# Tiles of 256 tokens with two neighbours in a partition, in a linear-attention and long-convolution kernel on one core

## The chip, the core and the metric

The kernel runs on one core of a Trainium2 chip. The core has five engines that run their own instruction queues and meet at semaphores: PE (TensorE, matrix products into PSUM), DVE (VectorE), ACT (ScalarE), POOL (GpSimd) and SP (SyncE, which here only issues DMAs). PSUM has eight banks of 512 fp32 columns in 128 partitions. DMA transfers are issued from the queues of SP and POOL. The metric is device microseconds of one execution; lower is better.

## The reference

A gated linear attention over 4 batches, 8 heads, 768 tokens and 48 channels, followed by a gated convolution over the whole sequence and a projection (d_model = 384 = 8 x 48):

```python
for t in range(S):
    cur = np.einsum('bhd,bhe->bhde', u[None] * kt, vt)
    y[:, :, t] = np.einsum('bhd,bhde->bhe', rt, state + cur)
    state = wt[:, :, :, None] * state + np.einsum('bhd,bhe->bhde', kt, vt)
...
x = attn_out.transpose(0, 2, 1, 3).reshape(B, S, H * D)
proj = x @ w_proj
x1, x2, x3 = (proj[..., :D].copy(), proj[..., D:2 * D].copy(), proj[..., 2 * D:].copy())
X2 = np.fft.rfft(x2, n=S, axis=1)
H = np.fft.rfft(filter_fft, n=S, axis=0)[None, :, :]
x2_conv = np.fft.irfft(X2 * H, n=S, axis=1)
y = x1 * x2_conv * x3
return (y @ w_out).astype(np.float32)
```

The term with `u` is the bonus: for each token and head it is a sum over the 48 channels of r*k*u, times v. All inputs and the output are fp32.

## The kernel before

The kernel has two stages for each of the four batches.

**First stage, by chunks of 128 tokens** (24 chunks, one token in a partition; `group` and `first`). w, r, k and v of a chunk are loaded by one DMA each, `[L, H, D]`, so each packet is one token of one head, 48 x 4 = 192 bytes (line 1438; twelve loads of v go through POOL's queue and are cast on the way, line 1435). ACT takes the logarithm of w (`ln`, line 1444), PE sums it over the tokens with two triangular masks (`cs`, lines 1473 to 1476), ACT takes exponentials in place in PSUM (`ex`, line 1482; `ph`, line 1493, for the decay over the chunk), and DVE multiplies them into k and r at once (`kq`, 768 columns, helper line 1328). PE turns the result (`tr`, line 1501; two heads to a transpose, each padded to 64 rows), ACT or DVE copies it to SBUF (`qk`), or SP turns it by DMA (line 1507, for the last eight chunks only, `late`). PE then forms the scores (`sc`, line 1519), which are masked by DVE in one product (`mt`, line 1535), or copied by ACT and cut by POOL (`mc`, line 1540). The state goes through PSUM: `ki` (line 1566) adds the old one by the identity, `kv` (line 1560) adds k times v, `su` (line 1570) applies the decay. The output of the chunk is a sum in PSUM of the bonus (`yi`, line 1580, by the identity; or it is added by DVE, line 1609), of r times state (`ys`, line 1589), and of masked scores times v (`yy`, line 1597). It is copied (`xn`), turned (`yt`, line 1621) and stored as `xT`, channels in partitions. The bonus's sum over the channels is made outside PE: `rk` (r*k), `ru` (times u), `rh` (first half plus second half) and a reduction `cc` (line 1458), then `vc` = v times it.

**Second stage, by batch** (`second`): gates x1 and x3 (`p`, `q`, line 1768), the side that is convolved (`xw`, line 1809), the forward transform of the sums and differences of its two halves (`sd`, `f`, line 1655), products with the filter's spectrum (`u`, `p`), the inverse transform (`E`, line 1865), whose even and odd parts are added and subtracted (`aE`, lines 1903 and 1908; `dE`, line 1918), the gate (`yE`), the output projection (`o`, line 1950) and the store (`so`, line 1966). The spectrum of the filter is made once. `PE`, `FOLD` are two ways of the inverse: with both halves in PE, or folded with a `dE` on DVE or POOL.

**Order.** The functions only declare operations with the engines that may do them; the order of all work, the engine of each operation and its PSUM bank stand in one list, `ORDER`, read line by line by `Plan.run`: name, engine (P, A, D, G, S; `-` leaves a variant out), bank. Each engine's queue is in this order; semaphores follow from the data. A last word on a line ties a POOL operation to a DVE operation that it must follow. `warm n bank` issues n filler products whose results are not used (line 1380); there are 93 such units.

Of the kernel before, what the change touches and what calls it, by code (L numbers as in the profile page):

```python
# [15 lines left out]
AX = mybir.AxisListType  # L16
# [4 lines left out]
L = 128  # L21
NCH = S // L
# [6 lines left out]
QT = HALF // 2  # L29
MID = (HALF - 1) / 4  # L30
NC = B * NCH
UNIT = 65536.0

PE, ACT, DVE, POOL, SP, NONE = "P", "A", "D", "G", "S", "-"


ADD, DVE2, ACT2, POOL2, FOLD, WIDE = "V", "M", "N", "C", "Q", "X"

NLW, NLD, NG, NF, NS, NX, NO = 3, 4, 3, 4, 3, 3, 4
CASTS = (2,4,6,8,10,12,)  # L40
NV, NVL = 6, 3
NTURN = 8
NE = 2


# [3 lines left out]
warm 16 4  # L49
first A  # L50
imaps G
smalls D
zeros D
pads D
signs D
lw0 S
lw3 S
kz1 D
ln0 A
maske G  # L60
lw2 S
lr0 S
u S
maskn G smalls
maps G
ang2 D
ia0.0 G
ia1.0 G
maski G
kz0 G pads  # L70
ang1 D
ang0 D
ia2.0 D
cs0 P 2
lk0 S
ln2 A
ex0 A
ew0 -
kq0 D
warm 8 0  # L80
warm 6 1
cs3 P 0
ex3 -
ia2.1 D
kw0 -
lw1 S
ur A
warm 4 5
um P 6
warm 5 5  # L90
tr0 P 4
lk3 S
lr3 S
ew3 X
lr1 S
lk1 S
kz2 G
ph0 A
ub A
ln1 A  # L100
lv0 S
rk0 G ang0
kz3 G kq0
ru0 G
rh0 D
cc0 D
qk0 A
kq3 -
kw3 G rh0
lv2 G cc0  # L110
warm 3 5
cs1 P 5
warm 3 7
sc0 P 3
mt0.1 D
mc0.1 -
lr2 S
lk2 S
vb0 G
vc0 G rh0  # L120
ex1 A
ph3 A
mt0.0 D
ew1 -
lv3 G
warm 3 7
cs2 P 0
warm 4 7
tr3 P 4
ex2 A  # L130
kq1 D
qk3 A
kw1 -
warm 2 7
tr1 P 7
mc0.0 -
rk1 D
ru1 D
rh1 G rk1
qk1 D  # L140
ph1 A
warm 3 2
sc3 P 4
kv0 P 2
su0 D
ew2 -
kq2 D
kw2 -
lv1 S
warm 2 3  # L150
sc1 P 6
yi0 P 2
y0 P
mt1.1 D
lw4 S
mt3.1 -
xn0 A
xa0 -
mt3.0 N
ph2 A  # L160
rk2 D
ru2 D
rh2 G rk2
vb1 A
tr2 P 3
warm 3 2
ki1 P 5
warm 2 2
kv1 P
lw5 S  # L170
lk4 S
lr4 S
qk2 A
ln3 A
mt1.0 D
cc1 D
yt0 P 2
lr5 S
lk5 S
lv5 S  # L180
warm 3 4
sc2 P 0
su1 D
warm 1 3
ki2 P 5
kv2 P
cc2 D
su2 D
cs4 P 6
ex4 A  # L190
wproj1 G
mc3.1 -
ki3 P 4
kv3 P
mt2.1 A
mc1.1 -
ia0.1 G
vc1 D
xT0 D
warm 2 3  # L200
yi1 P 2
ys1 P
vc2 G
mt2.0 D
mc1.0 -
y1 P
ew4 -
su3 D
mc2.1 G mt1.0
kq4 D  # L210
mc2.0 -
cs5 P 0
xn1 A
ex5 A
warm 1 4
yi2 P 3
ys2 P
y2 P
kw4 -
kq5 D  # L220
ew5 -
lw7 S
ph4 A
xn2 A
tr4 P 6
xa1 -
xa2 -
kw5 -
qk4 D
yt1 P 3  # L230
tr5 P 2
yi3 P 6
qk5 D
yt2 P 4
ph5 A
wproj0 G kq4
mc3.0 C
lv4 S
xT2 D
ys3 P  # L240
lr7 S
y3 P
xn3 D
sc4 P 4
mt4.0 D
xa3 -
trig A
sin2 A
rk3 G qk4
ru3 G qk5  # L250
warm 1 0
yt3 P 7
xT1 D
mt4.1 A
ia1.1 G mt4.0
warm 3 0
sc5 P 5
mt5.1 -
lw6 S
mt5.0 M  # L260
xw0.0 P 0
rh3 D
cc3 D
vb3 G rh3
sin1 A
vc3 G mt5.0
ki4 P 2
cxw0.0 D
xT3 A
warm 1 3  # L270
xw0.2 P 6
sin0 A
kv4 P
is A
cxw0.2 D
su4 D
warm 5 4
p0.2.0 P 5
p0.0.0 P 0
table A  # L280
lr6 S
lk6 S
lk7 S
mc4.1 G
filt S
lw8 S
lw9 S
cp0.0.0 D
yi4 P 6
yi5 P 2  # L290
ys5 P
lv7 G cxw0.2
mc5.0 -
mc5.1 -
ys4 P
y5 P
lk9 S
lk8 S
mc4.0 -
y4 P  # L300
xn4 D
if1 A
ln4 A
xn5 A
lv8 S
cs6 P 0
xa5 -
yt5 P 3
if0 A
ex6 A  # L310
lr9 S
xa4 -
yt4 P 2
xT5 D
xT4 D
cs7 P 6
ew6 -
kq6 D
ex7 A
ew7 -  # L320
xw0.4 P 2
lr8 S
kq7 D
ph6 A
cxw0.4 A
sd0.1.0 D
kw7 -
sd0.0.0 D
rk4 G
p0.2.1 P 4  # L330
cp0.2.1 A
ph7 A
kw6 -
lw10 S
p0.0.1 P 0
tr7 P 3
qk7 D
fsd0 D
fsd1 D
tr6 P 7  # L340
ru4 D
cp0.0.1 A
qk6 A
cp0.2.0 A
lv9 S
f0.2 P 0
cf0.2 A
sc6 P 6
mt6.1 -
mc6.1 -  # L350
mt6.0 N
f0.0 P 4
sc7 P 2
cf0.0 A
warm 2 0
h1 P 0
ln5 A
lv6 G sd0.1.0
h2 P 6
rh4 G fsd1  # L360
mt7.1 -
mt7.0 M
mc7.0 -
hc1 A
mc7.1 -
cc4 D
h0 P 2
hc2 A
kv6 P 4
hg1 D  # L370
hg2 D
hc0 A
cs8 P 0
su6 D
mc6.0 C
vc4 G
warm 2 5
yi6 P 6
y6 P
ex8 A  # L380
ew8 -
hg0 D
xn6 A
yi7 P 4
ys7 P
y7 P
xn7 A
xa7 -
xa6 -
cs9 P 6  # L390
kq8 D
yt6 P 3
ki7 P 2
kv7 P
su7 D
wproj2 G
yt7 P 4
xT7 D
ex9 A
xT6 A  # L400
kq9 D
kw8 -
rk5 G
ph8 A
ru5 D
rh5 D
cc5 D
ew9 -
tr8 P 5
ki8 P 2  # L410
qk8 A
ph9 A
vb5 G xT7
vc5 G
xw1.0 P 0
cxw1.0 A
kw9 -
tr9 P 3
qk9 A
kv8 P  # L420
sc8 P 4
su8 D
mt8.1 -
lw11 S
f0.1 P 0
ki9 P 6
kv9 P
mt8.0 M
if2 A
lk10 S  # L430
lk13 S
mc8.0 -
cf0.1 A
sc9 P 2
su9 D
q0.2.1 P 7
lr10 S
mt9.0 N
lk11 S
lr11 S  # L440
mt9.1 -
mc9.1 -
q0.0.1 P 5
lr13 S
yi9 P 0
q0.2.0 P 4
yi8 P 2
xq0.0.1 -
u10.0 D
lw12 S  # L450
ys9 P
ln6 A
ys8 P
cq0.0.1 D
lw13 S
mc8.1 -
y8 P
lv11 G su9
mc9.0 C
warm 5 2 192  # L460
y9 P
cs10 P 5
lr12 S
lv12 S
xq0.2.1 -
u00.0 D
xq0.2.0 -
xn8 A
xn9 A
q0.0.0 P 2  # L470
cq0.2.0 D
cq0.2.1 D
xq0.0.0 -
xa8 -
lk12 S
lv10 G
rk6 G
cq0.0.0 D
xa9 -
gq0.0.0 -  # L480
yt9 P 4
ex10 A
xT9 A
ru6 D
kq10 D
yt8 P 7
xT8 A
cs11 P 0
ex11 A
if3 A  # L490
kq11 D
warm 1 4
xw1.2 P 2
ew10 -
kw10 -
lk15 S
lv13 S
rh6 G ru6
cc6 D
ph10 A  # L500
lr15 S
gq0.2.0 -
lw15 S
lr14 S
p1.2.0 P 4
tr10 P 7
p1.0.0 P 5
cxw1.2 A
qk10 A
ew11 -  # L510
kw11 -
ph11 A
cp1.2.0 A
cp1.0.0 A
tr11 P 2
q1.0.0 P 0
ki10 P 3
sc10 P 4
xq1.0.0 -
ln7 A  # L520
p0.0 D
lw14 S
mt10.1 A
gq0.0.1 -
qk11 D
sc11 P 6
kv10 P
lv15 G
mt11.0 A
vc6 G  # L530
mc10.1 G kq11
mc11.0 G qk11
q1.2.0 P 2
xq1.2.0 -
cq1.0.0 D
mt10.0 D
mt11.1 D
cs12 P 0
rk7 G qk11
ru7 G  # L540
yi10 P 4
ex12 A
ew12 -
su10 D
lv19 G qk11
ys10 P
mc10.0 -
y10 P
lv14 G
mc11.1 -  # L550
cs13 P 6
gq0.2.1 -
# [1496 lines left out]
```

## Time and profile before

| | before |
|---|---|
| median of 3 runs | 158.71 us (158.08 to 159.05) |
| span of the profiled execution | 155.3 us; its own time was not recorded apart from the runs |
| busy, DVE / ACT / POOL | 135.5 / 117.5 / 102.0 us |
| PE products / DVE / ACT / POOL instructions | 1634 / 258 / 195 / 106 |
| HBM read and written | 22.41 and 4.72 MB |

The runs lie 2.8 to 3.8 us above the span, which goes from the first to the last instruction. The profile's page gives the load of each engine in 40 slices of the span, the chain of work that ended last, and the instructions grouped by line and shape. In a group's row, "xN | busy, mean" are the number of instructions, the time in which at least one of them ran, and the mean length of one; after the second bar stands the idle time of the engine just before them and what ended it. PE's products overlap, so their lengths add up to more than the time they take; the timeline gives their starts.

### The profile page before, as it was taken

Reading aid. Unit: us, or ns where it says so; the run is one execution under the profiler, and the core shown is the slowest. Engines: PE = TensorE matmul, PEld = TensorE weight load, DVE = VectorE, ACT = ScalarE, POOL = GpSimd, SP = SyncE. Lnnn points to the kernel's source line nnn. Section 1 sums busy time; section 2 is a strip of 40 time slices with the busy share of each in tenths; the row PEclk is TensorE's granted clock in tenths of the full one; section 3 lists DMA queues with packets and bytes.
Section 4 is the critical chain, followed back from the end, with each engine's and each line's share of the span. In section 5 each row is a group of like instructions: output and inputs, shape, how many; then the busy total and the mean of one; then the engine's idle time right before and its main releaser. Section 6 shows DMA issues by size and latency. Waiting matters only on the chain.

```text
span 155.3 us, 4220 instructions
## 1 busy us (share of the span) xinstructions
PE 142.3 (92%) x1634; PEld 89.4 (58%) x1634; DVE 135.5 (87%) x258; ACT 117.5 (76%) x195; POOL 102.0 (66%) x106
## 2 busy tenths in 40 slices
PE   7999894999999999999799999999999997999860
PEld 2455554656646767666566676665666664666430
DVE  4849984696999998999999999999999988799950
ACT  4584774897899894999879989989965575667650
POOL 6679595968229479589957988678796650802600
PEclk9999999699999999999999999999999999999997
DMA  5999999979999999899999918999997535000784
GB/s 105 227 212 218 194 145 215 200 135 339 177 187 213 198 181 180 142 199 176 187 192 201 179 25 144 220 193 189 178 183 149 155 122 209 0 0 34 294 330 159
DMA packets 112534, 27.12 MB, mean 175 GB/s; under 512 B 108545, under 2 KB 111106, under 8 KB 112514
## 3 DMA queue, kind: packets, MB, share of 16 engines
q1 hardware_dynamic: 98434, 24.49, 73.9%
q0 software_dynamic: 14080, 2.36, 20.0%
q8 instruction: 13, 0.21, 0.6%
q14 instruction: 7, 0.06, 0.1%
HBM read 22.41 MB, written 4.72 MB: 175 GB/s over the span
## 4 chain that ended last, share of the span: by engine, by line
PE 65%; DVE 11%; DMA 9%; ACT 4%; SPq 4%; issue 2%; DVEq 0%; ACTq 0%
PE banks L1768 13%; PE banks L1655 10%; PE banks L1380 7%; PE banks L1809 6%; PE banks L1950 5%; DMA kr<-in_k_dram 4%; PE banks L1865 4%; PE banks L1501 4%; SPq L1438 4%; PE banks L1519 4%; PE banks L1597 3%; DMA w<-in_w_dram 3%; DMA xT<-xn 3%; PE banks L1589 2%; PE banks L1473 2%
## 5 line engine op out<-in xcount | busy, mean ns | idle before, releaser
L1768 PE MATMUL banks<-xT,wproj 128*128 128x384 bf16 x144 | 27.3, 326 | 1.1 <-DVE xT L1334 1.0
L1328 DVE TENSOR_TENSOR kq<-banks,kr 128x768 bf16<-128x768 f32 x23 | 21.6, 950 | 3.1 <-DMA kr<-in_k_dram 2.7
L1328 POOL TENSOR_TENSOR vc<-vb,cc 128x768 bf16<-128x768 bf16 (+1 forms) x12 | 18.7, 1562 | 6.0 <-DVE sd L1820 3.1
L1328 POOL TENSOR_TENSOR rk<-kr 128x768 bf16<-128x768 f32 (+1 forms) x11 | 19.5, 1773 | 4.1 <-DMA kr<-in_k_dram 2.1
L1332 ACT ACTIVATE x<-banks 128x768 bf16<-128x768 f32 (+1 forms) x26 | 17.5, 687 | 5.2 <-PE banks L1809 3.0
L1482 ACT ACTIVATE banks<-banks 128x768 f32<-128x768 f32 x23 | 18.2, 798 | 1.9 <-PE banks L1476 1.6
L1535 DVE TENSOR_TENSOR mt<-banks,mask_excl 128x512 bf16<-128x512 f32 (+1 forms) x24 | 18.1, 772 | 1.3 <-PE banks L1519 1.1
L1768 PEld LDWEIGHTS <-wproj 128*128 128x128 bf16 x144 | 13.5, 98 | 9.3 <-issue 1.2
L1380 PE MATMUL banks<-wt 128*128 128x512 bf16 (+1 forms) x56 | 16.9, 397 | 1.1 <-DVE scl L1394 1.1
L1809 PE MATMUL banks<-wproj,xT 128*128 128x384 bf16 x72 | 13.7, 326 | 1.5 <-DMA xT<-xn 1.0
L1435 POOL DMA_DIRECT2D vb<-in_v_dram x12 | 11.3, 938 | 4.6 <-DVE sd L1820 3.3
L1540 POOL TENSOR_SCALAR_AFFINE_SELECT mt<-mt 128x512 bf16<-128x512 bf16 (+1 forms) x14 | 11.6, 834 | 3.5 <-ACT mt L1332 3.5
L1950 PE MATMUL banks<-wout,y 128*128 128x384 bf16 x72 | 13.3, 326 | 0.7 <-DVE y L1328 0.4
L1655 PE MATMUL banks<-sd,F 128*128 128x384 bf16 (+1 forms) x96 | 13.7, 328 | 0.0
L1501 PE MATMUL banks<-ident,kq 128*128 128x128 bf16 x144 | 11.1, 222 | 2.6 <-DVE kq L1328 2.1
L1332 ACT ACTIVATE qk<-banks 128x1024 bf16<-128x1024 bf16 x12 | 12.3, 1023 | 1.1 <-PE banks L1501 0.9
L1444 ACT ACTIVATE lg<-w 128x768 bf16<-128x768 f32 (+1 forms) x13 | 10.4, 798 | 3.2 <-DMA w<-in_w_dram 3.1
L1455 POOL TENSOR_TENSOR rk<-rk 128x384 bf16<-128x384 bf16 (+1 forms) x8 | 7.4, 921 | 7.7 <-DVE rk L1328 7.6
L1332 ACT ACTIVATE X<-banks 128x768 bf16<-128x768 f32 x12 | 9.8, 815 | 3.0 <-PE banks L1655 2.9
L1501 PEld LDWEIGHTS <-kq 128*128 128x128 bf16 x144 | 9.0, 98 | 4.9 <-DVE kq L1328 2.9
L1655 PEld LDWEIGHTS <-F 128*128 128x128 bf16 (+1 forms) x120 | 8.4, 103 | 5.6 <-issue 1.0
L1328 DVE TENSOR_TENSOR U<-X,hh 128x2304 bf16<-128x2304 bf16 (+1 forms) x12 | 11.6, 982 | 0.0
(118 smaller groups left out, 338.3 us busy)
## 6 DMA issues: line engine op xcount, KB each, us to landing
w<-in_w_dram SPq DMA_DIRECT2D x24, 192.0 KB, 4.2
kr<-in_r_dram SPq DMA_DIRECT2D x24, 192.0 KB, 4.5
kr<-in_k_dram SPq DMA_DIRECT2D x24, 192.0 KB, 4.5
out_dram<-o SPq DMA_DIRECT2D x9, 384.0 KB, 2.9
v<-in_v_dram SPq DMA_DIRECT2D x12, 192.0 KB, 4.0
vb<-in_v_dram POOLq DMA_DIRECT2D x12, 96.0 KB, 5.5
U<-in_moe_filter_fft_dram SPq DMA_DIRECT2D x1, 1152.0 KB, 6.0
wproj<-in_moe_w_proj_dram POOLq DMA_DIRECT2D x3, 288.0 KB, 5.1
```

The source lines that it names most:

```text
L1328: return eng(e).tensor_mul(o, a, b)
L1332: return nc.scalar.activation(out=o, in_=a, func=AF.Copy)
L1380: nc.tensor.matmul(banks[:, at, lo:hi], wt[:, 0:L], x, start=True, stop=True)
L1435: op(f"lv{i}", [POOL], lambda e, bk, q=q, rw=rw: nc.gpsimd.dma_start(out=vb[fv][:, q], in_=v[b, :, rw, :].rearrange("h t d -> t h d")), w= ...
L1482: return nc.scalar.activation(out=o, in_=x, func=AF.Exp)
L1501: nc.tensor.transpose(p[:, HP * m + j, :], kq[f][:, m, 2 * j:2 * j + 2, :], ident)
L1535: return copy(ACT, o, x) if e in (ACT, ACT2) else nc.vector.tensor_mul(o, x, _mid(mask_excl, z - HP * a))
L1540: return nc.gpsimd.affine_select(out=o, in_=o, pattern=[[0, z - HP * a], [1, L]], compare_op=ALU.is_gt, fill=0.0, base=0, channel_multipli ...
L1655: nc.tensor.matmul(p[rows], F[:, ti, c0 + rows.start:c0 + rows.stop], x[q][:, ti, :], start=(ti == 0), stop=(ti == NT - 1),)
L1768: nc.tensor.matmul(p, wproj[:, cb, col0:col0 + L], xT[bx][:, cb, sl], start=(cb == 0), stop=(cb == CB - 1),)
L1809: nc.tensor.matmul(view(bk)[:, z], xT[bx][:, cb, (c0 + z) * L:(c0 + z + 1) * L], wproj[:, cb, C:2 * C], start=(cb == 0), stop=(cb == CB - 1),)
L1950: nc.tensor.matmul(view(bk)[:, z], yt_[:, z, :], wout[:, cb, :], start=(cb == 0), stop=(cb == CB - 1),)
```

## The change

- A tile holds 256 tokens (12 pairs, function `pair` in place of `group` and `first`), two neighbouring tokens j = 0, 1 in each partition. A load of w, r, k or v is then one DMA of 1024 packets of 2 x 48 x 4 = 384 bytes; no load of v is cast on the way.
- A partition group of 64 holds a chunk of 128 tokens: partitions 0 to 63 the first chunk, 64 to 127 the second. The running sums need the even and odd token apart: DVE or POOL forms w_even * w_odd (`ws`), the masks `before` and `upto` are block-diagonal 64 x 64, and `cs` is four wide products for 256 tokens (six for the one pair without `ws`), in three banks.
- k is scaled by exp of the negative sums from SBUF (`ek`, `km`, on DVE or POOL), q from PSUM (`eq`, `qm`).
- State, state read, scores and bonus are products with 64 rows and 64 columns of the array; masked scores times v have 64 rows and 128 columns. There are twice as many of each per token, of the same width (scores: 128 columns, half of which are the even and half the odd tokens).
- The bonus: r*k (`rk`) is turned (`rp` on PE and `rt` as a copy, or `rt` by DMA), and six products with a matrix of u and zeros give its sums over the channels (`cp`, copied by `cc`). `ru`, `rh` and the reduction go.
- The masking is one product on DVE, from PSUM (15 of 24) or from a copy made by ACT (9).
- Turns by DMA: 16 of 24 output tiles, 13 sets of q or k, 4 of r*k (before: 5 and 6).
- The second stage keeps its form; its sequence axis is ordered with even tokens first and odd tokens second (`j`), through gates, inverse tables and output; the forward tables are made for the new order of rows. The gates may be copied by ACT and multiplied from SBUF. Eight of nine inverse sums of the first three batches are folded, before four.
- The order list is new. The tables of sines and the loading of ACT's function tables stand ahead of the first logarithm. There are 49 filler units, 43 of them ahead of the first `cs`.

The core of the diff:

```diff
-    wl = tiles(NLW, [L, 2, H, D], FP32, "w")
-    kr = tiles(NLD, [L, 2, 2, H, D], FP32, "kr")
+    wl = tiles(NW, [L, H, 2, D], FP32, "w")
+    kr = tiles(NR, [L, 2, H, 2, D], FP32, "kr")
...
+        def load(name, t, x, key):
+            op(f"l{name}{gi}", [SP], lambda e, bk: nc.sync.dma_start(
+                out=t.rearrange("p h j d -> p h (j d)"),
+                in_=x[b, :, rows, :].rearrange("h (p j) d -> p h (j d)", j=2)), w=[key], q=(1024, 384))
...
+            if both(bk):
+                sums = (((before, le), (before, ls)), ((upto, le), (before, ls)), ((upto, le), (upto, ls)))
+            else:
+                sums = (((before, ls),), ((before, ls), (ident, le)), ((upto, ls),))
...
-                    nc.tensor.matmul(
-                        p[:, par, j, :], qk[f][p0:p0 + D, j, :], qk[f][p0:p0 + D, HP + j, :],
-                        start=True, stop=True,
-                    )
+                                nc.tensor.matmul(
+                                    p[spans[c], par, i, jk, :].rearrange("p (j t) -> p j t", j=2),
+                                    qkk[x, 0, jk, 2 * a + i, spans[c]], qkk[x, 1, :, 2 * a + i, spans[c]],
+                                    start=True, stop=True,
+                                )
...
+                                nc.tensor.matmul(
+                                    kvp(bk)[spans[par], hp, :], kqq[spans[c], 0, j, h, :], vbb[spans[c], h, j, :],
+                                    start=(ci == 0 and hp == 0 and j == 0), stop=(hp == HP - 1 and j == 1),
+                                )
...
+                                nc.tensor.matmul(
+                                    yview(bk, c)[spans[j], par, hp, :], qkk[x, 1, j, hp, spans[c]], stt[so][x, hp, :],
+                                    start=hp == 0, stop=False,
+                                )
...
+                            nc.tensor.matmul(
+                                yview(bk, c)[:, par, hp, :], mt[sm][spans[c], a, par, q, jk, :],
+                                vbb[spans[c], 2 * hp + par, jk, :],
+                                start=(pi == 0 and c == 0 and hp == 0 and jk == 0), stop=False,
+                            )
...
+        def bonus(e, bk):
+            p = one(bk, f"cp{gi}")[:, 0:2 * H]
+            for n in range(6):
+                nc.tensor.matmul(p, rt[srk][:, n, :], u_b[:, n, :], start=n == 0, stop=n == 5)
```

2759 lines of the change are left out of this document (1288 added, 1471 removed).

## The prediction

> **What bounds the kernel now.** I read the page first, for the loads of the engines and of the transfer queues.
>
> ```profile
> span 155.3 us, 4220 instructions
> PE 142.3 (92%) x1634; PEld 89.4 (58%) x1634; DVE 135.5 (87%) x258; ACT 117.5 (76%) x195; POOL 102.0 (66%) x106
> ...
> PEclk9999999699999999999999999999999999999997
> DMA  5999999979999999899999918999997535000784
> ...
> q1 hardware_dynamic: 98434, 24.49, 73.9%
> q0 software_dynamic: 14080, 2.36, 20.0%
> ```
>
> Three resources are nearly full at once: PE, DVE and, until about 120 us, the DMA engines, which are kept busy by small packets (112,514 packets for 27 MB). A share over the span does not say which one sets the end, so I took the busy time by stage next, for everything and then for line 1380 alone, the filler products ("warm") whose results nobody reads.
>
> ```profile
> 0.00:32.00 32.00, 27.80 (x295) 15.82 (x296) 23.25 (x66) 21.05 (x35) 24.16 (x42) 0.95 1.12 191
> 32.00:150.00 118.00, 114.36 (x1339) 73.62 (x1338) 111.65 (x192) 95.87 (x161) 77.89 (x64) 1.00 0.92 168
> 150.00:156.00 6.00, 0.18 (x2) 0.00 (x0) 0.56 (x1) 0.54 (x1) 0.00 (x0) 0.75 0.49 189
> ```
>
> ```profile
> 0.00:32.00 32.00, 14.06 (x44) 4.10 (x44) 0.95 1.12 191
> 32.00:150.00 118.00, 2.85 (x12) 1.00 (x12) 1.00 0.92 168
> ```
>
> The columns are PE, PEld, DVE, ACT, POOL, the granted clock, the DMA share and GB/s; the second block has PE and PEld only. Without filler PE does 27.80 - 14.06 = 13.7 us of work in the first 32 us, 114.36 - 2.85 = 111.5 us in the next 118, and nothing to speak of in the last 5.1 us (from 150.2 to 155.3), which are the last copies and the store. That is 125.4 us of real PE work. So the run is a start of 32 us that is mostly waiting, a dense stage in which PE works 94.5% and DVE 94.6% of the time, and a fixed end. What counts is PE's real work, how early it becomes dense, and how dense it can stay.
>
> **PE's products, priced.** A busy PE overlaps its products, so I price them from start to start in the timeline (columns: start, length, count).
>
> ```profile
> 36.04 0.37 PE L1589 MATMUL banks<-S,qk 48*128 48x48 bf16 x16
> 36.34 0.57 PE L1597 MATMUL banks<-vb,mt 128*128 128x48 bf16 x16
> 36.83 0.34 PE L1473 MATMUL banks<-lg,mask_neg 128*128 128x384 bf16 x1
> ...
> 37.30 0.61 PE L1621 MATMUL banks<-ident,xn 128*128 128x128 bf16 x6
> ...
> 52.48 1.14 PE L1809 MATMUL banks<-wproj,xT 128*128 128x384 bf16 x6
> 53.46 0.61 PE L1501 MATMUL banks<-ident,kq 128*128 128x128 bf16 x8
> 54.00 0.31 PE L1560 MATMUL banks<-vb,kq 128*64 128x48 bf16 x8
> 54.24 0.40 PE L1519 MATMUL banks<-qk 48*128 48x128 bf16 x8
> 54.57 1.17 PE L1655 MATMUL banks<-sd,F 128*64 128x384 bf16 x12
> ```
>
> A 384-wide product costs 0.98/6 = 0.163 us, a transpose 0.54/8 = 0.067, the running sums of a chunk (cs) 37.30 - 36.83 = 0.47. The small ones: state into kv 0.24 for 8, scores 0.33 for 8, state read (ys) 0.30 for 16, mask times v (yy) 0.49 for 16. A whole-array product of 48 columns thus takes 31 ns, one on half of the rows 19 ns: halves do overlap. No row shows a product on a quarter of the array.
>
> The change per 256 tokens. cs: four wide and four narrow products for two chunks' eight and eight: about 0.65 + 0.14 = 0.79 instead of 0.94; times 12, plus 0.5 for the one pair that sums both tokens on PE, -1.3. Transposes of q and k: 11 sets of eight are left on PE of 18, -7 x 0.54 = -3.8; of the output, 8 sets of three instead of 19, -11 x 0.20 = -2.2; new ones of r*k for the bonus, 8 x 6 x 0.067 = +3.2; the bonus sums, 72 narrow products at about 0.035 (the four narrow ones are the last 0.14 of cs), +2.5. The state product becomes 16 small products for 8, on one half of the rows and alternating column halves as now: between 0.24 (all hidden) and 0.48 (doubled); I take 0.37, since the pace within a run of eight is below the 0.03 that includes the change of shape: 20 x 0.13 = +2.6. ys becomes 16 for 8: 0.30 by its own row against 0.20 (0.30 less half of sixteen at that pace, and the change of shape stays), 20 x 0.10 = +2.0; bounds 0 and +5.8 (31 ns each). Scores: 16 quarter products for 8 half ones, on four quarters that write different banks or halves of them; I take the same 0.33, as for halves the pace halved with the part of the array; bounds 0 and 24 x 0.21 = +5. yy: 32 half products for 16 whole ones, same 0.49; upper bound +5.9. The bonus added by the identity: 24 wide-equivalents at 0.08 to 0.12 for 32, -0.8; if its quarters do not overlap, +1.9. The inverse transform: four of nine that were six 384-wide sums go folded (two 384, four 192 wide), 4 x 2 x 0.163 = -1.3. The sum is -1.3 - 3.8 - 2.2 + 3.2 + 2.5 + 2.6 + 2.0 - 0.8 - 1.3 = +0.9: PE's real work stays at **126.3 us**, with bounds of about 122 and 145. Sixteen of the 24 output transposes and 17 others move to DMA, so PE is where the gain is spent again.
>
> **DVE, ACT, POOL, DMA.** Grouped by form:
>
> ```profile
> L1328 DVE TENSOR_TENSOR kq<-banks,kr 128x768 bf16<-128x768 f32 x23 | 21.6, 950 | 3.1 <-DMA kr<-in_k_dram 2.7 <-ACT banks L1482 0.2
> L1535 DVE TENSOR_TENSOR mt<-banks,mask_excl 128x512 bf16<-128x512 f32 x20 | 13.2, 682 | 0.4 <-PE banks L1519 0.4
> ...
> L1458 DVE TENSOR_REDUCE cc<-rk 128x16 f32<-128x384 bf16 x11 | 6.0, 545 | 0.1
> ...
> L1535 DVE TENSOR_TENSOR mt<-banks,mask_excl 128x1024 bf16<-128x1024 f32 x4 | 4.9, 1221 | 0.9 <-PE banks L1519 0.7
> ...
> L1328 DVE TENSOR_TENSOR y<-y,g 128x768 bf16<-128x768 bf16 x8 | 4.5, 598 | 0.0
> L1328 DVE TENSOR_TENSOR rk<-rk,u_b 128x768 bf16<-128x768 bf16 x7 | 4.5, 640 | 0.0
> ...
> L1455 DVE TENSOR_TENSOR rk<-rk 128x384 bf16<-128x384 bf16 x4 | 3.1, 769 | 0.0
> ...
> L1328 DVE TENSOR_TENSOR rk<-kr 128x768 bf16<-128x768 f32 x1 | 0.9, 948 | 0.0
> ```
>
> DVE: q and k scaling 16 products of 768 for 23, -7 x 0.95 = -6.7 (eight more go to POOL). Masking 15 of 1024 from PSUM (1.22) and 9 from SBUF (about 0.72, the 598 ns row taken to 1024) = 24.8 for 13.2 + 4.9 = 18.1, +6.7. The bonus by VectorE goes (4.5 + 3.1 + 6.0), and four turns of about 0.5 and two tiny copies come, -11.3. Five more r*k, +4.7. Gating mostly from SBUF, about -4; fewer turns and copies, about -7; nine more foldings at 0.35, +3.2; squares of w, flips and small ones, +5. About **-9 us**. ACT gains 14 gating copies (about 9) and casts of v, loses turns and flips: about +5. POOL loses the masking, the bonus and the twelve casting loads: down by some 20.
>
> DMA: 48 loads of 1024 packets of 384 B for 96 of 192 B. A packet now costs 0.739 x 155.3 x 16 / 98434 = 18.7 ns of an engine; the twelve loads of the first batch then need between 14.4 us (same price per packet) and 24.7 us (4.72 MB at the 191 GB/s of the first stage). I take 17, nearer to the packet's price, since the share is full at only 191 GB/s. The 2.7 us that DVE waits for k in the row above go. The cover would be gone only above 25 us, because by then ACT is later, as follows.
>
> **The start.** Rows for ACT:
>
> ```profile
> L1482 ACT ACTIVATE banks<-banks 128x768 f32<-128x768 f32 x23 | 18.2, 798 | 1.9 <-PE banks L1476 1.6
> L1332 ACT ACTIVATE qk<-banks 128x1024 bf16<-128x1024 bf16 x12 | 12.3, 1023 | 1.1 <-PE banks L1501 0.9
> ...
> L1672 ACT ACTIVATE F<-o,mpi 128x768 bf16<-128x768 uint16 x3 | 2.8, 931 | 0.0
> ...
> L1661 ACT ACT_TABLE_LOAD x1 | 1.3, 1283 | 0.8 <-PEq L2033 0.8
> ```
>
> The trigonometric tables move to the front: three table loads (3.85), three sines (2.8) and a wide one (about 1.3) from 0.8 us on, and some waiting for DVE's angles, so the first logarithm starts at about 9.5 us; PE fills that with 22 warm products. Up to the first product of the second stage ACT then does 12 logarithms and exponentials at about 0.8 (9.6), 4 small ones (0.7), 6 turns at 1.02 (6.1), three of 768 (2.4), a mask copy (1.0), three casts (2.5), and three copies and three tiny ones (2.0): 24.3, less 0.05 of overlap for each of 35, 22.5. The second stage starts at 32.0 plus 1.5 of waits, 33.5 us, hardly other than now. But ahead of it stand in the new order the products of three whole pairs and of much of the fourth, by the prices above 20.4 us against 13.7 now, and ACT's 8 us of tables are behind it. Fillers go from 93 to 49 units, 43 of them before the first sum. The row of the clock has one slice at 0.6 now, in the start; two such slices of 3.9 us would cost the new start 3 us, which I keep for the range only, because PE has 20.4 us of work there.
>
> **The sum.** 126.3 - 20.4 = 105.9 us of PE work are left at 33.5 us. DVE has 9 us less to do, POOL 20, DMA is free; ACT's share stays near 81%. I let PE work 96% of the time instead of 94.5%: 110.3 us. With the end of 5.1 us the span is 33.5 + 110.3 + 5.1 = 148.9 us. The runs (158.08 to 159.05, median 158.71) lie 3.4 us above the profiled span, so the time is 152.3, **152 us**.
>
> **The rivals.**
> *Better than that*: quarters overlap four deep and PE's work falls to 122; at 98% in the dense stage that is 33.5 + 103.7 + 8.5 = 145.7 us. 8%.
> *The gain is hidden or given back, about 159*: either only two of four quarters run together (scores +5, identity +1.9, 7 / 0.96 = 7.3, 159.6), or the turns by DMA come late:
>
> ```profile
> xT<-xn SPq DMA_TRANSPOSE x5, 3.9
> ```
>
> SP's queue holds loads and turns in one order, so a turn that waits for its xn holds the loads behind it; three batches that each wait 2.4 us for their last turn give 159.5. Against it: other batches' work stands between. 13%.
> *Slower, by banks*: a pair holds four PSUM banks from its first state read until its output copies, its sums take three and each half of its scores two, where eight exist and a chunk now needs two, two and two. PE then waits for the mask product of 1.22 us that frees the scores. One us in each of 12 pairs gives 164; it decides above 0.7 us a pair. For it: PE already waits nowhere long, so the order is tight; against it: DVE has more room. 13%.
> *Slower, by small products*: every small product costs a whole one's 31 ns: state 0.49 (+2.4), ys 0.49 (+3.8), scores (+3.8), yy 0.98 (+5.9), together 15.9 / 0.96 = 16.6, 169 us. The 19 ns of ys speak against it. 8%. [...]
>
> **Chances.** Forecast 58%. One per cent is about what a measurement of this kernel can tell from no change: 157.1 to 160.3. Faster 58 + 8 = 66%, the same 11% of the 13, slower 2 + 13 + 8 = 23%. The range of 146 to 164 leaves out most of the better case, the 169 and the upper half of the banks' case, about 20%; the forecast's own range is 146 to 157.
>
> **What would show it.** Right: real PE work (without line of the warm products) of 122 to 130 us; 16 scores in 0.3 to 0.4 us from start to start; DVE near 127; first logarithm near 9.5 us, second stage near 33.5; DMA share well below 0.9. Wrong: PE idle before scores or state reads for a mask product (banks), for xT (turns), small products at 25 to 31 ns each, or a second stage that begins after 38 us.

## The result: slower by 8%, and the profile after

| | forecast | before | after |
|---|---|---|---|
| time, median of the runs (us) | 152 | 158.45 (158.08 to 159.05) | 171.84 (169.48 to 176.97) |
| ratio to before, 95% interval | 0.96 | | 1.080 (1.071 to 1.089) |
| start: time without real PE work, up to the first product of the second stage (us) | 13.1 | 18.0 | 15.2 |
| PE's real work (us) | 126.3 | 125.4 | 133.1 |
| dense stage: time without real PE work (us) | 4.4 | 6.8 | 16.2 |
| end, after PE's last product (us) | 5.1 | 5.1 | 5.7 |
| span of the profiled execution (us) | 148.9 | 155.3 | 170.2 |

The profiled execution of the changed kernel took 171.99 us, 1.8 us more than its span. Runs more than 1.5% above a kernel's fastest are left out of every ratio here, so that a ratio can be missing or differ from that of the medians. Each experiment's ratio is to the kernel before as it ran in the same session (medians of 158.77 to 160.66 us); the changed kernel itself was timed in one session only, the one of this table.

The page of the changed kernel, engines and slices:

```profile
span 170.2 us, 5650 instructions
...
PE 140.2 (82%) x2371; PEld 90.2 (53%) x2371; DVE 128.7 (76%) x248; ACT 123.3 (72%) x196; POOL 75.8 (45%) x84
...
PEclk9978997899999999699999999999659999999997
DMA  5999979976999999989899999999912201321884
```

DVE and POOL have less to do than before, ACT about as much as foretold, and every engine works a smaller share. Ahead of the end the granted clock dips in seven slices instead of one, and the DMA engines are nearly full up to 123 us. The stages, split at the first product of the second stage and at PE's last product (columns: stretch, length, PE's busy time and products, clock, DMA share, GB/s), after, and its filler products alone:

```profile
0.00:39.68 39.68, 30.82 (x658) 0.91 0.91 238
39.68:164.50 124.82, 109.39 (x1714) 0.96 0.81 173
164.50:170.20 5.70, 0.00 (x0) 0.80 0.54 174
```

```profile
0.00:39.68 39.68, 6.29 (x22) 0.91 0.91 238
39.68:164.50 124.82, 0.81 (x3) 0.96 0.81 173
```

The same two for the kernel before:

```profile
0.00:30.65 30.65, 26.46 (x288) 0.94 1.12 189
30.65:150.20 119.55, 115.88 (x1351) 1.00 0.92 169
```

```profile
0.00:30.65 30.65, 13.79 (x43) 0.94 1.12 189
30.65:150.20 119.55, 3.12 (x13) 1.00 0.92 169
```

Real work is the first number less the fillers: 24.53 us in the start and 108.58 in the dense stage, where 124.82 us pass; PE is 87.0% dense there. Before it was 112.76 in 119.55, 94.3%. The table is made of these rows. (In the kernel before, real products start while a filler's recorded time still runs, so that this subtraction is some 2 to 5 us too large there; the runs without fillers below have the work with nothing to subtract.) Against the forecast's span 21.3 us are lost: 11.8 as waits in the dense stage, 6.8 as longer PE work, 2.1 in the start, 0.6 at the end.

What PE waits for in the changed kernel (engine and line, what ended the wait: us in total, times, longest). Line 1286 is the product of q (`qm`), 1258 the running sums (`cs`), 1333 the sums of the bonus, 1381 the state reads (`ys`), 1400 the scores, 1631 the gates:

```profile
PE banks L1258 <- DVE kq L1286: 5.8, 5, 2.4
PE banks L1258 <- ACT lg L1245: 3.4, 1, 3.4
PE banks L1333 <- DMA rt<-rk: 3.2, 1, 3.2
PE banks L1381 <- DVE kq L1286: 2.3, 2, 1.4
PE banks L1381 <- issue: 1.9, 1, 1.9
PE banks L1631 <- DVE kq L1286: 1.7, 2, 1.2
PE banks L1400 <- DMA qk<-kq: 0.8, 1, 0.8
...
PE banks L1631 <- DVE mt L1084: 0.4, 1, 0.4
```

The q product ends 9.8 us of PE's waits, 8.0 of them in the dense stage, the mask product 0.4, turns by DMA 4.0. PE never waits for a turned output (`xT`). Three of the longest groups of the kernel before, whose one long wait (1.83 us) lies in the start:

```profile
PE banks L1501 <- DVE kq L1328: 2.1, 2, 1.8
...
PE banks L1809 <- DMA xT<-xn: 1.0, 1, 1.0
PE banks L1768 <- DVE xT L1334: 1.0, 1, 1.0
```

The longest wait for the q product, in the timeline (start, length, instruction, and in brackets the idle time before it):

```profile
64.37 0.80 ACT L1276 ACTIVATE banks<-banks 128x768 f32<-128x768 f32 x1
...
65.16 0.95 DVE L1084 TENSOR_TENSOR kq<-xk,kr 128x768 bf16<-128x768 f32 x1
...
66.03 0.95 DVE L1089 CAST X<-banks 128x768 bf16<-128x768 f32 x1
...
66.89 0.95 DVE L1286 TENSOR_TENSOR kq<-banks,kr 128x768 bf16<-128x768 f32 x1
67.14 1.81 POOL L1084 TENSOR_TENSOR rk<-kr 128x768 bf16<-128x768 f32 x1
67.89 0.49 PE L1258 MATMUL banks<-lg,before 128*128 128x384 bf16 x2 [2.43 <-DVE kq L1286]
```

The sums of pair 7 take the three banks of pair 6 (`cs6 P 4` and `cs7 P 4` in the order list; so do pairs 4 and 5, 8 and 9, 10 and 11). They are free when q of pair 6 has been multiplied out of them. Its exponential ends at 65.17 us, but DVE has two other instructions in its queue first (65.16 and 66.03 us), and PE, for which these sums come next in the list, stands for 2.43 us.

In this trace the granted clock is 1.00 or 0.50, and its records last 3.41 us or a multiple of that (up to 47.79 us). Three pairs of neighbouring windows of 3.41 us (PE's busy time and products, clock, DMA share, GB/s; the page shows 1.00 ahead of the first record of the clock, which begins at 4.13 us here):

```profile
7.54:10.96 3.42, 0.13 (x1) 1.00 1.07 285
10.96:14.37 3.41, 3.41 (x24) 0.50 1.11 304
65.57:68.98 3.41, 1.08 (x24) 1.00 0.93 229
68.98:72.40 3.42, 3.42 (x34) 0.50 1.34 156
116.77:120.18 3.41, 1.82 (x69) 1.00 1.43 178
120.18:123.60 3.42, 1.84 (x27) 0.50 0.95 195
```

After each of these windows, in which PE worked little, comes one at half clock: behind the start, behind the wait just shown, and in one of 3.2 us for the last turn of r*k. There are five ahead of PE's last product, before there was one. The other two begin at 123.60 us, after the window at 120.18, and at 28.02, after a window in which PE was busy for 2.50 of 3.41 us, with 117 small products; so PE's busy time alone does not sort the windows, and a later run comes back to it. The longest pause of PE in the first window of the second pair was 2.43 us. The trace puts 15.3 us of real PE work into the five windows. A wide product of the sums takes 0.32 us from start to start there (30.04 to 30.36 us) and 0.16 at full clock (68.38 to 68.54), 32 products of masked scores and v 0.75 (123.31 to 124.06) and 0.50 (below). By the author's estimate, with everything taken to double as the wide ones do, half of the 15.3, 7.7 us, is what the windows add, against 1.8 before, and at full clock PE's work is 133.1 - 7.7 = 125.4 us.

The small products, by their starts:

```profile
55.05 0.44 PE L1381 MATMUL banks<-S,qk 48*64 48x48 bf16 x32
55.31 0.41 PE L1400 MATMUL banks<-qk 48*64 48x128 bf16 x16
55.65 0.66 PE L1486 MATMUL banks<-sd,F 128*128 128x384 bf16 x3
```

```profile
40.81 0.57 PE L1422 MATMUL banks<-vb,mt 64*128 64x48 bf16 x32
41.31 0.36 PE L1436 MATMUL banks<-vc,ident 64*64 64x192 bf16 x8
```

32 state reads in 0.26 us (8 ns each), 16 scores in 0.34, 32 products of scores and v in 0.50. The transfers that turn tiles (count, median from issue to landing):

```profile
xT<-xn SPq DMA_TRANSPOSE x16, 3.3
qk<-kq SPq DMA_TRANSPOSE x13, 4.6
rt<-rk SPq DMA_TRANSPOSE x4, 4.2
```

33 turns for 11. Added up over the trace's packets, the work of the 16 DMA engines on loads of w, r, k and v fell from 109.1 to 75.6 us, that on turns rose from 11.0 to 36.9.

### The profile page after: what moved, and what is told of

Read it like the earlier page. It is cut to its first block, busy times and chain, and to the rows that moved or that the text cites. A ratio compares the mean times of both kernels' runs of the same rounds, so it can differ in the third digit from the quotient of the medians.

```text
span 170.2 us, 5650 instructions
## 1 busy us (share of the span) xinstructions
PE 140.2 (82%) x2371; PEld 90.2 (53%) x2371; DVE 128.7 (76%) x248; ACT 123.3 (72%) x196; POOL 75.8 (45%) x84
## 4 chain that ended last, share of the span: by engine, by line
PE 34%; DVE 13%; DMA 4%; ACT 2%; issue 2%; SPq 1%; ACTq 0%; DVEq 0%
PE banks L1631 8%; PE banks L1793 7%; PE banks L1486 7%; PE banks L1722 4%; DMA rt<-rk 4%; DVE U L1084 3%; DVE kq L1286 3%; PE banks L1655 2%; DVE mt L1084 2%; PE banks L1258 1%; DVE P L1695 1%; PE banks L1422 1%; DVE sd L1667 1%; DVE S L1372 1%; PE banks L1361 1%
## 5 line engine op out<-in xcount | busy, mean ns | idle before, releaser
L1084 DVE TENSOR_TENSOR mt<-banks,causal 128x1024 bf16<-128x1024 f32 x15 | 18.1, 1218 | 6.2 <-PE banks L1400 6.2
L1084 POOL TENSOR_TENSOR vc<-vb,cc 128x768 bf16<-128x768 bf16 x10 | 14.7, 1474 | 16.6 <-ACT xn L1088 10.2
L1084 POOL TENSOR_TENSOR kq<-xk,kr 128x768 bf16<-128x768 f32 x8 | 14.5, 1810 | 16.7 <-DVE U L1084 12.2
L1267 ACT ACTIVATE xk<-banks 128x768 f32<-128x768 f32 x12 | 9.7, 812 | 7.7 <-PE banks L1262 7.7
L1793 PE MATMUL banks<-wout,y 128*128 128x384 bf16 (+1 forms) x78 | 13.3, 327 | 0.0
L1286 DVE TENSOR_TENSOR kq<-banks,kr 128x768 bf16<-128x768 f32 x12 | 11.4, 951 | 1.6 <-ACT banks L1276 1.5
L1088 ACT ACTIVATE o<-banks 128x768 f32<-128x768 f32 (+1 forms) x12 | 9.0, 760 | 4.1 <-PE banks L1793 3.8
L1084 POOL TENSOR_TENSOR rk<-kr 128x768 bf16<-128x768 f32 x6 | 10.9, 1817 | 1.4 <-DMA kr<-in_k_dram 1.4
L1400 PE MATMUL banks<-qk 48*64 48x128 bf16 x384 | 10.2, 221 | 1.3 <-DMA qk<-kq 0.8
L1088 ACT ACTIVATE xn<-banks 128x384 bf16<-128x384 f32 x20 | 9.0, 490 | 2.4 <-PE banks L1436 2.3
```

The lines of the kernel that those rows point to most:

```text
L1084: return eng(e).tensor_mul(o, a, b)
L1088: return nc.scalar.activation(out=o, in_=a, func=AF.Copy)
L1267: op(f"ek{gi}", [ACT], lambda e, bk: nc.scalar.activation(out=xk[sx].rearrange("p j h d -> p j (h d)"), in_=three(bk, f"cs{gi}")[:, 1:3, 0 ...
L1286: op(f"qm{gi}", [DVE], lambda e, bk: nc.vector.tensor_mul(kqq[:, 1, :, :, 0:D], three(bk, f"cs{gi}")[:, 0:2, 0:C].rearrange("p j (h d) -> ...
L1400: nc.tensor.matmul(p[spans[c], par, i, jk, :].rearrange("p (j t) -> p j t", j=2), qkk[x, 0, jk, 2 * a + i, spans[c]], qkk[x, 1, :, 2 * a + ...
L1793: nc.tensor.matmul(view(bk)[:, j] if full else view(bk)[spans[j]], y[cb][:, j, p0:p0 + m], wout[:, cb, :], start=(cb == 0), stop=(cb == CB ...
```

## The experiments

Three explanations stood against each other: the banks that wait for the q product, the turns by DMA with the loads behind them, and the clock. Letters in the expectations stand for these and for variants of them.

**The q product freed from the banks.** ACT writes the exponentials to an SBUF tile of their own, and the banks are free 0.95 us or more earlier (the unused tile `mf` makes room).

```diff
+    xq = tiles(NX, [L, 2, H, D], FP32, "xq")
...
-            return nc.scalar.activation(out=p, in_=p, func=AF.Exp)
+            return nc.scalar.activation(out=xq[sx].rearrange("p j h d -> p j (h d)"), in_=p, func=AF.Exp)
...
-            kqq[:, 1, :, :, 0:D], three(bk, f"cs{gi}")[:, 0:2, 0:C].rearrange("p j (h d) -> p j h d", h=H),
-            jhd(kr[sr][:, 1])),
+            kqq[:, 1, :, :, 0:D], xq[sx], jhd(kr[sr][:, 1])),
```

> The exponential of q's sums (eq) is written to SBUF instead of in place, so the three banks of cs come free after ACT and not after DVE's product (qm); nothing is left out. Theory W (PE, in order, waits for qm of the pair before, 10 us of its 30 us of idle time): the waits of PE for line 1286 go (cs5, cs7, cs9, cs11) and the time falls by 7 us or more, to 165 or less. Theory D (transfers are late: DMA is 0.9 and more busy until 123 us): under 2 us, 170 to 172, and PE waits for something else in the same places. Theory B (both stand in series, each behind the other): 3 to 4 us, 168.

169.95 us (167.68 to 176.46), ratio 1.053 (1.046 to 1.059). No wait of the sums for the q product is left. The time is nearest to that of theory B. PE's idle time between its products fell from 23.1 to 19.4 us only, since other waits grew, those for turns from 4.0 to 4.5 us among them. Part of the gain went into the product itself (first row after, second this run: count, busy time, mean ns):

```profile
L1286 DVE TENSOR_TENSOR kq<-banks,kr 128x768 bf16<-128x768 f32 x12 | 11.4, 951 | 1.6 <-ACT banks L1276 1.5
```

```profile
L1287 DVE TENSOR_TENSOR kq<-xq,kr 128x768 bf16<-128x768 f32 x12 | 13.8, 1158 | 0.6 <-ACT xq L1277 0.6
```

With both operands in SBUF the mean is 1.16 us for 0.95; the shortest of the twelve takes 0.95, the longest 1.63. What makes the long ones long these rows do not show.

**Fewer loads.** Eight of the twelve loads of v are left out.

```diff
-lv4 S
+lv4 -
...
-lv11 S
+lv11 -
```

> The loads of v of the last eight pairs are left out (older values are used), 8 of 48 loads of 1024 packets; nothing else changes. Theory D: DMA is what binds, its share falls and the turns and the loads of k, r, w land earlier, time down by 5 us or more, to 167. Theory W: 171 to 172, no change. Theory B: 2 to 3 us, about 169.

170.94 us (169.18 to 173.88), ratio 1.061 (1.055 to 1.067): by the ratios, transfers that have nothing to do with the turns are worth 1.9% too, which speaks against DMA engines that are free. PE's waits for turns fell with them, from 4.0 to 3.0 us.

**Fewer turns.** 28 of the 33 turns are left out.

```diff
-ck5 S
+ck5 -
...
-rt8 S
+rt8 -
...
-xT18 S
+xT18 -
```

> 28 of the 33 turns by DMA are left out (13 of q and k, 4 of r*k, the 11 of the outputs of the last two batches; older values are used), with no PE work in their place. Theory D in the form that the turns themselves are late (their transfer and 1.25 us of SP's issue each): down by 7 us or more, to 165, and no wait of PE for a turn is left. Theory W: under 2 us, 170 to 172. Theory B: 3 to 4 us, 168.

167.86 us (167.44 to 168.41), ratio 1.049 (1.045 to 1.054). This is theory B's number. The waits for turns are gone, those for the q product stand as they were (5.8, 2.3 and 1.7 us). The run leaves five turns where the kernel before has eleven, and it relieves SP's queue and the DMA engines at once, so it does not say which of the two counts, nor is all of it owed to the added turns. The profile has six windows in a row at half clock, from 24.5 to 44.9 us.

**Both.** The edits of the first and the third run together.

> Both edits: eq to SBUF, and the 28 turns left out. Theory B: together far more than the sum of the two alone, 12 to 17 us, 155 to 160, and at most two windows of 3.4 us at half clock in place of five. Theory W alone: as q_from_sbuf. Theory D alone: as fewer_turns.

163.72 us (162.78 to 164.43), ratio 1.023 (1.018 to 1.029). From 1.080 the two alone take off 0.027 and 0.031, together 0.057: separate causes that add up, and no more. The hope of 155 to 160 was missed; three windows stand at half clock, not two, and the q product grew to 1.35 us here. The profiles add up in another way than the times. PE's idle time between its products is 23.1 us after the change, 19.4 with the q product freed, 16.6 with fewer turns and 16.3 with both; its real work is 133.1, 131.6, 136.3 and 131.3 us. What the second edit adds to fewer turns is thus not less waiting, but less work at half clock (26.6 us of it with fewer turns, 10.0 with both). How much of the two gains comes by way of the clock is not separated.

**Another order.** The same instructions on the same engines, in an order and with banks found by a search in a model of the queues; in the second about 60 operations change their engine as well.

```diff
-cs6 P 4
+cs6 P 3
...
-cs7 P 4
+cs7 P 5
```

> The changed kernel with another order: the same instructions on the same engines, the same buffers and the same 49 filler units, only the order in the list and the PSUM bank of each tile are others, found by a search in a model of the queues with the durations of the traced run. Theory O (the new tiles cost nothing by themselves; the order and the banks make PE wait, and the waits halve the clock): the model gives 155 us of span without any window at half clock, against 171 for the order of the change, so about 157 us, 14 us less than after. Theory L (the tiles themselves bound it: chains of 256 tokens, small products, packets): 167 us or more, as whatever is cleared in one place is waited for in the next. Theory D (DMA's load binds): 165 or more, for every load and turn is still there.

> As reordered, but the search may also choose the engine of copies, masks, scalings and turns (DVE, ACT, POOL, SP; every operation stays). The model gives 150.4 us of span, about 152 us. Theory O: 150 to 155, below the kernel before. Theory L: 165 or more.

174.67 us, ratio 1.100 (1.091 to 1.109), and 180.23, ratio 1.133 (1.124 to 1.142), not 157 and 152. PE's waits between products did fall in the first (17.1 us for 23.1 in after), but other work took their place that the model did not know, of which one case in the timeline:

```profile
72.05 1.80 POOL L1084 TENSOR_TENSOR rk<-kr 128x768 bf16<-128x768 f32 x1
72.11 2.56 DVE L1084 TENSOR_TENSOR kq<-xk,kr 128x768 bf16<-128x768 f32 x1
```

The k product, which took 0.95 us at 65.16 us of after with POOL idle, takes 2.56 beside r*k on POOL and ends 0.8 us after it. The last word of some lines in the order of after keeps such pairs apart.

**Fillers where PE waits.** About 140 filler units spread over the waits of after.

```diff
+warm 14 1
...
-warm 43 3
...
+warm 10 4
```

> The changed kernel with its own order and banks; only filler products differ: some 140 units spread over the waits in place of 49. Theory C (a stretch of 3.4 us in which PE is busy for less than about half is followed by 3.4 us at half clock, and five of these cost after some 5 us on the path): no or one window at half clock, and the span 4 to 5 us shorter, about 167 us. If the clock's loss is hidden behind the waits: 171 or 172. If the fillers themselves delay PE: 173 or more.

174.52 us (172.78 to 176.14), ratio 1.094 (1.083 to 1.105), not 167; four windows stay at half clock. **No fillers at all**, in both kernels:

```diff
-warm 43 3
...
-warm 6 5
```

> The kernel before with its 93 filler units left out, nothing else. Theory C: several windows at half clock in the first 35 us, where PE does 13.7 us of work in 32, and 2 to 6 us more than before, 160 to 164. If the clock doesn't depend on PE's activity, or its loss is hidden: 157 to 159.

> The changed kernel without its 49 filler units, nothing else. Theory C (fewer products lower the clock and the clock sets the time): more windows at half clock, 174 or more. Theory N (as for the kernel before, whose time fell by 2% without fillers: in the start PE waits for ACT, DVE and the loads, and neither fillers nor the clock set its end): 168 to 172.

Before without fillers: 155.25 us (154.95 to 157.10), ratio 0.979 (0.970 to 0.988), the fastest kernel of this study, against an expectation of 160 to 164. Its first record of full clock comes at 30.3 us: eight transposes take 0.90 us at 9.06 us and 0.85 at 28.49 for the 0.54 of before, and six wide products from 32.14 us on take 0.99 (0.98 in before, at 52.48). 20 us of its PE work are done ahead of that record, at half clock by these rows, and yet it loses nothing: that work lies in a start that waits anyway (5.7 us of PE's waits are for the first logarithms). Why it gains 2% was not tried. After without fillers: 175.55 us, ratio 1.095 (1.084 to 1.106), not to be told from after with certainty.

**Order again**, by a search in the model of the queues with other assumptions and without fillers; in the second also `xq`, other engines and 18 turns instead of 33.

```diff
-cs7 P 4
...
-warm 43 3
...
+cs7 P 2
```

> The changed kernel with another order and other banks, without fillers; the same instructions on the same engines and the same buffers. [...] It gives 157 us of span (after's order by the same model: 171 to 174). Theory O (the order and the banks cost it, not the tiles): 163 or less. Theory L (the tiles themselves): 168 or more.

> As reordered_2, with eq to SBUF, and with engines chosen anew: 18 turns by DMA in place of 33 (15 go to PE with a copy), masks, copies and scalings spread otherwise. The model gives 152 us of span. Theory O with T (waits for the banks, for turns, and the order together are the whole loss): 154 to 159, at or below the kernel before. Theory L: 165 or more.

175.84 us (171.65 to 177.17), no ratio, and 182.67, ratio 1.150 (1.141 to 1.158). In the first only 15.3 us of waits are left between PE's products, the first of which starts at 12.3 us, but 33.0 us of work lie at half clock (the profiled execution took 177.17 us); in the second the q product takes 1.54 us. Neither says what a good order of the new tiles would give; that stays open.

**Three fillers** ahead of the three longest waits:

```diff
+warm 16 2
 ys11 P 2
...
+warm 20 7
 cs7 P 4
...
+warm 28 4
 cp11 P 4
```

> The changed kernel with three filler runs more, each put where its PE waits longest in the dense stage and as long as the wait (1.7 us ahead of ys11, 2.1 us ahead of cs7, 3.0 us ahead of cp11), in banks that are free; nothing else. In the profile of after these waits stand before three of its windows at half clock (69.0, 120.2 and 123.6 us). Theory C (waits lower the clock of the next 3.4 us, and that costs 1.7 us each on the path): no half window there, and 4 to 5 us less, 167. Theory H (the clock's loss is hidden by other waits): 171 to 172. If the fillers end after what PE waited for: 173 or more.

178.11 us (173.52 to 178.97), no ratio. The windows at half clock of 68.98, 120.18 and 123.60 us are gone (68 to 72 and 116 to 124 us stand at 1.00), and there is no gain. In the profile, of an execution of 177.63 us, the wait marked "issue" grew from 1.9 to 3.7 us, the four fillers from 63.49 us on, behind it, are 0.46 us apart, where those at full clock are 0.22, and in the start some products of the sums take 0.32 us (16.92 and 29.27 us) for 0.16; the mean clock rose from 0.943 to 0.951 only.

**What the clock counts, in the start.** Small fillers (64 x 64, 48 columns) ahead of the first sums against whole ones of the same number of units.

```diff
-warm 43 3
+warm 80 3
...
+            for _ in range(4):
+                for a, b in ((0, 0), (0, 1), (1, 0), (1, 1)):
+                    nc.tensor.matmul(banks[spans[b], at + a, 128 * a:128 * a + 48], wt[spans[a], 0:DP], wt[spans[a], 0:48],
+                                     start=True, stop=True)
```

> The changed kernel; the fillers ahead of the first sum are small products (64 rows, 64 columns of the array, 48 wide, four quarters in turn, 640 of them, about 9 us) in place of 22 whole-array ones of 512 columns. Theory Q (small products hardly count as work for the clock): PE is busy ahead of the first sum, and yet the clock isn't at full speed before the whole-array products come, the first record of full clock comes after 11 us. Rival (any busy PE counts): full clock after about 4 us, as in after. Its time isn't of interest.

> The control for start_small: 80 filler units (40 whole-array products of 512 columns, about 9.5 us) ahead of the first sum in place of 43. Theory Q and its rival both: full clock from about 4 us on, and no half window between 4 and 14 us.

188.01 and 178.15 us, one run each. The small ones came in blocks of 128 with four pauses of 2.4 to 2.9 us, so that PE was not busy and the question was not answered. The profile names nothing that PE waits for in these pauses ("issue").

**The q product first in DVE's queue.** Pairs 5, 6, 9 and 10, no operand changed.

```diff
+qm6 D
 km6 D
...
 cf0.0 D
-qm6 D
...
 qm10 D
+km10 D
+vb10 G km10
```

> Only VectorE's order is changed: in pairs 5, 6, 9 and 10 the q product is put ahead of one or two instructions that do not free a bank (in pair 6 ahead of the k product and of a copy). In the profile of after the q products of these pairs started 1.10, 1.72, 0.62 and 0.63 us after their exponentials had ended, 4.1 us together; all other pairs lose less. If the wait is for the banks that the q product frees, and its length is a matter of VectorE's order, PE's waits for the q product fall from 9.8 us to 6 or 7, and the time falls by 3 to 4 us, to 166 to 169 us (ratio 1.05 to 1.065), and unlike the run with the q product from SBUF, no q product becomes longer than 0.96 us. If the delay of the k product, the copy and the sums that are now behind it is worth as much, other waits of PE grow by the same and the time stays at 170 to 172.

> The same order, and the 28 late turns by DMA left out (their results are stale tiles, so part of the work is left out). If banks and turns are separate causes, the two gains add: 171.8 - 3.5 - 4 = 164 to 165 us. If the turns' effect on the time was mostly that a late q product also issues its turn late, the gain is smaller than the sum: 166 to 167, near to the run with fewer turns alone (167.9).

Alone 176.11 us (171.37 to 178.47), no ratio: a gain is not shown. PE's longer waits in its profile, of an execution of 176.87 us, without those for turns:

```profile
PE banks L1381 <- issue: 3.0, 1, 3.0
PE banks L1258 <- DVE kq L1286: 2.4, 3, 1.3
PE banks L1381 <- DVE kq L1286: 2.3, 2, 1.4
```

The sums now wait 2.4 us for the q product instead of 5.8, as expected, but one wait for a turn of r*k takes 3.8 us, and nine windows stand at half clock, five of them from 26.7 us on. With the turns left out too: 164.13 us (162.44 to 164.86), ratio 1.024 (1.014 to 1.034), inside the range for causes that add up: 3.7 us less than with fewer turns alone.

**The early stretch at half clock.** In that run the clock is down in seven windows in a row, 21.45 to 45.35 us, although PE is busy (the page's row of the clock, then four of the windows, columns as above):

```profile
PEclk9987965555599999999999999999999999999997
```

```profile
24.87:28.28 3.41, 3.41 (x123) 0.50 1.10 297
28.28:31.69 3.41, 2.70 (x21) 0.50 1.09 286
...
35.11:38.52 3.41, 3.41 (x96) 0.50 0.29 78
38.52:41.93 3.41, 3.26 (x93) 0.50 0.23 15
```

34 units of wide fillers were put there, and as a control narrow ones of the same PE time by the author's estimate.

```diff
+warm 8 1
 ys1 P 4
...
+            elif z < n - 100:
+                for _ in range(6):
+                    nc.tensor.matmul(banks[:, at, 0:2], wt[:, 0:L], wt[:, 0:2], start=True, stop=True)
```

> The kernel is the one with the q product first and the 28 late turns left out (164.13 us); 34 filler units, 17 products of the whole array with 512 columns, are spread over 20 to 41 us, of which 8 units lie in a wait of 1.4 us. At full clock they are 17 x 0.21 = 3.6 us of PE time, 2.7 of it not in a wait. In the profile without them seven windows of 3.41 us in a row, from 21.45 to 45.35 us, stand at half clock, although PE is busy in 0.79 to 1.00 of each: if the clock follows whole-array work (small products counting little), these fillers keep it up there, the first product of the second stage (43.70) comes at 40 to 41 us, PE's work at half clock falls from 26 us to 12 or less, and the time to 160 to 162. If the clock does not follow them, or the start waits for other engines anyway, the second stage starts no earlier and the time is 164 to 167.

> The control for the run with 34 whole-array filler units: the same places, but each product of 512 columns is replaced by six products of 2 columns, which take about the same PE time (four such take 0.14 us in the sums of a chunk) and do little work in the array. If the clock follows the time that PE is busy, this run is like the one with wide fillers. If it follows the work in the array, the seven windows stay at half clock and the time is 164 to 167 us, 3 us or more above the run with wide fillers.

The rows of the clock, wide, then narrow:

```profile
PEclk9999699999999985899999999999999999999998
```

```profile
PEclk9999975598699999999999999999999999999996
```

Wide fillers keep the clock up between 19 and 60 us, narrow ones leave four windows of that stretch at half: from 24 to 45 us PE is busy for 19.64 of 21 us at a clock of 1.00 with wide ones, and for 19.88 with narrow ones, at 0.50, 0.87 and 0.76 in the three stretches of 7 us. The second stage starts at 39.85 us (wide), 42.64 (narrow), 43.70 (none), as the theory had it. But the times are 165.12 us (165.09 to 167.08; ratio 1.044, 1.029 to 1.059) and 164.17 (163.96 to 164.46; ratio 1.034, 1.027 to 1.042), no better than 164.13. In the run with wide fillers the lead of 3.9 us is gone at the sums of pair 6 (65.13 us for 65.49); in between PE stands:

```profile
57.09 0.27 PE L1443 MATMUL banks<-vc,ident 64*64 64x192 bf16 x2
60.17 0.53 PE L1443 MATMUL banks<-vc,ident 64*64 64x192 bf16 x6 [2.81 <-issue]
```

and two windows at half clock follow. The profile names no cause of this pause.

## Why the prediction was wrong, step by step

- *PE's work, 126.3 us*: right. 125.4 at full clock, by the estimate above. In the two runs without fillers it is 135.9 us before, 20.2 of them at half clock, and 134.6 after, 19.0 of them at half: 125.8 and 125.1 at full clock by the same estimate, so that the change itself costs PE next to nothing. The state reads were cheaper than allowed, scores and masked scores as said. The rival of the small products at 31 ns falls: 8 to 21 ns from start to start in these rows.
- *DVE near 127, ACT +5, POOL -20*: 128.7, +5.8 and -26.2; right for DVE and ACT, and POOL lost more than foreseen.
- *First logarithm at 9.5 us*: 9.94. *Loads of 17 us*: eleven of the twelve had landed at 17.3 us by the trace. *Second stage at 33.5*: 39.68, beyond the 38 us that the prediction had named as a sign against it. PE had done 24.5 us of work by then for the 20.4 foreseen, 6.7 of it at half clock; time without work cost 2.1 us more than foreseen.
- *"DMA is free"*: wrong. The price of a load was near (17 us for twelve is 22.1 ns a packet, the trace has 24.6; the 18.7 ns of before mix all packets, those of 192 bytes took 16.1), but the 22 added turns were not put into the sum; they took back 25.9 of the 33.5 us that the loads gave, and the DMA share of the dense stage fell from 0.92 to 0.81 only. The rival that turns come late was held to the end of giving the gain back; leaving 28 turns out is worth 3.1%, about 5 us, and the turns that PE waits for are those of r*k and k or q, not the rival's `xT`.
- *"I let PE work 96% of the time"*: the step that failed, 11.8 of the 21.3 us. It was 87.0%: of the 16.2 us without real work PE waits 8.0 for the banks that the q product frees, 4.0 for turns by DMA and 1.9 with no cause in the profile. The forecast had taken the 94.5% of before and raised it for the lighter loads of DVE and POOL; a lighter DVE (128.7 us for 135.5) did not help where its queue puts other work ahead of the instruction that PE stands for. The rival of the banks had the kind of wait and the size (9.8 us are 0.8 a pair, above its 0.7), but the wrong owner: the q product, not the mask product (0.4 us), and it was given 13%. Undoing it is worth 2.7%, or 3.7 us by DVE's order where the turns are out of the way.
- *Half clock "for the range only"*: by the estimate 5.9 us more than before, a term that the forecast put at nothing in the dense stage. As a cause of the time it is not shown: with the clock kept up in three windows of the dense stage (three fillers) or in the early stretch (wide fillers) the time did not fall. Nor is it ruled out, since these fillers take PE time of their own and a longer pause came with each of them (3.7 us for 1.9, and 2.8 for 0.7). Four of the five windows of the changed kernel follow one in which PE was busy for 1.84 of 3.41 us or less. Without fillers 20.2 us of the work of before lay at half clock and the time was 2% shorter; where half clock costs time no run shows.
- *3.4 us outside the span*: 1.8 in the profiled execution. In a later session the kernel before, too, had 1.7 (160.12 us for a span of 158.4); the 3.4 probably came from setting runs against the span of another execution.

Undoing the waits for banks and leaving out turns takes away 5.7 of the 8.0%, though the second leaves out work. What remains, 2.3%, and the forecast's 4% below before stay unsettled: PE's pauses without a named cause, the clock and the other waits lie in it, and the orders tried here were no better than that of the change.

## What to carry to other kernels

Work out who frees a bank last and what stands ahead of that instruction in its own queue, for every tile whose successor uses the same bank; here PE stood still for 9.8 us in all for the q products in DVE's queue. Put every transfer into the sum of the DMA engines, turns as well as loads, before one calls them free. Try a tuned kernel without its fillers: here that alone, at 155.25 us, beat both.

## What the runs showed of the hardware

- In these runs the granted clock did not go by PE's busy time alone: with the q product first and fewer turns, windows at half clock in which PE is busy for 3.41 of 3.41 us are followed by others at half (rows above). In the two runs with early fillers PE is busy for nearly the same time from 24 to 45 us, 19.64 us at a clock of 1.00 throughout with fillers of 512 columns, 19.88 at 0.50, 0.87 and 0.76 with fillers of 2 columns.
- A DVE product with two SBUF operands took 2.56 us beside a POOL instruction (the k product in the first other order) and 0.95 with POOL idle (65.16 us of after). A product with one operand in PSUM took 0.95 beside POOL's r*k (66.89 and 67.14 us in the timeline above). These are single cases.
- SP's issue of one turn by DMA lasts 1.2 to 3.6 us in after (median 1.25 of the 33; one of an output tile from 125.53 to 126.71 us, and the next begins at 126.76).
- The page of after counts 18 transfers of 16 KB on a queue of kind "instruction", that of before 13. PE's pause of 1.9 us in after, from 57.98 us, begins while one of them runs (57.42 to 58.55 us); whether the one causes the other no run shows.
